# Moving attention probabilities into place inside SBUF instead of through DRAM, in a PE-bound three-stage kernel

## The chip, the core and the metric

The kernel runs on one NeuronCore of a Trainium2 chip. The metric is the device time of one execution in microseconds (us). A run of the profiler gives, beside that, a trace of every instruction; its clock starts at the first instruction of the program, and the time from there to the last is called the span.

## The reference

Three stages follow each other. The first is attention within chunks of 64 rows (8 batches, 8 heads, 576 rows, head size 64); its output becomes a matrix x of 4608 rows and 512 columns. The second is a feed-forward layer with a softplus, the third one with a maximum over three products.

```
scores = scale * np.matmul(q_c, k_c.transpose(0, 1, 2, 4, 3))      # 64 x 64 per chunk
scores = scores - np.max(scores, axis=-1, keepdims=True)
attn = np.exp(scores)
attn = attn / (np.sum(attn, axis=-1, keepdims=True) + 1e-09)
out = np.matmul(attn, v_c)
...
x = np.ascontiguousarray(attn_out.transpose(0, 2, 1, 3)).reshape(B * S, H * D)
h = x @ w_in                                  # 4608 x 512 by 512 x 2048
x = (np.maximum(h, 0.0) + np.log1p(np.exp(-np.abs(h)))) @ w_out
h = np.maximum(np.maximum(x @ w1, x @ w2), x @ w3)   # three times 512 x 768
out = h @ w_out
```

## The kernel before

The 4608 rows are nine blocks of 512. A block of x is made from four attention tiles, one for each pair of heads, so there are 36 tiles; the first eight (`attention_first`) run at the start, the other 28 (`attention`, tiles 8 to 35) are spread between the matmuls of the second stage. Blocks 0 to 2 go through that stage directly (`mlp1`, matmuls on lines 807 and 839); blocks 3 to 8 go in pairs with fewer, prepared products (`UnitA` on line 1135, `mlp1_out` on 1434, `Sevens` on 1280 and 1357). The third stage (`Triple`, lines 1582 and 1680) closes the program. The weights of the later products are sums and differences that the kernel computes itself and keeps in DRAM: `combos` writes them as `wso` (POOL, line 1248), `weights3` as `w2c` (POOL, line 940).

Nothing in the program order is written by hand. Every piece of work is an operation with a cost, a due time, what it reads and writes, and a latency `lat`; `Plan.order` runs through a model of the engines, always takes the waiting operation with the earliest due time, chooses between VectorE and ScalarE for the copies that may run on either, and hands out buffers as the model says they come free. The order in which operations start in that model is the order in which each engine's queue is filled. A change of one cost or latency therefore moves many instructions and changes which buffer each one gets. The large SBUF buffers are 46 places, s0 to s45, of 128 partitions by 4 KB; a name such as s14_268 is place s14, and 268 the running number of the buffer that got it.

In `attention`, tile t loads q, k and v (lines 445 and 470, on SP and POOL), transposes q and k on VectorE (lines 700, 701), and then one group of small TensorE matmuls, `products` (line 505, and 599 in the later tiles, which are called with `apart`), does two things: the scores of tile t and the product of the probabilities of tile t-2 with its v. The softmax follows on VectorE and ScalarE (line 564 and around it). The probabilities then have to be transposed. VectorE's transpose (line 753) does it within blocks of 32 by 32 and writes the lower half `pt` of a buffer PT; blocks that belong in another group of 32 partitions have to be carried there. Before the change `pt` is stored to a DRAM tile `pd` (line 757) and read back into the upper half `pT` by four loads, one for each group of 32 partitions (line 762), all issued by SP. `products` of tile t+2 reads `pT` and v.

Every queue runs its instructions in order: a DMA that waits on SP or POOL holds back all that stands behind it there, and a cast that waits on ScalarE all casts behind it.

Of the kernel before, what the change touches and what calls it, by code (L numbers as in the profile page):

```python
# [185 lines left out]
def tile_kernel(ctx: ExitStack, tc: tile.TileContext, q, k, v, w_in, w_out, w1, w2, w3, wo2, out):  # L186
    nc = tc.nc
    B, H, S, D = q.shape
# [3 lines left out]
    CH = 64  # L192
# [4 lines left out]
    TB = 512  # L197
    NB = NT // TB
    NC = TB // CH
    NTILE = NB * HP  # L200
# [68 lines left out]
    def slot(*kinds, shape=[P, 2, TB], dt=F32R):  # L269
        return Buf(*kinds, fresh=lambda i: slot_at(i, shape, dt))  # L270
# [5 lines left out]
    op = plan.op  # L276

    def copy_op(dst, src, r, w, psum=False, n=1.0, engs="DA", **kw):
        cost = {"D": 0.69 if psum else 0.43, "A": 0.58 if psum else 0.62}

        def fn(e):
            if e == "A":
                nc.scalar.copy(dst(), src())  # L283
            else:
                nc.vector.tensor_copy(dst(), src())

        return op({e: cost[e] * n for e in engs}, fn, r=r, w=w, **kw)
# [399 lines left out]
    def attention(t, after=(), apart=False):  # L687

        if t < NTILE:
# [4 lines left out]
            QK = slot("qh", "z", dt=F32)  # L694
# [8 lines left out]
        old = before.pop(0) if len(before) == 2 or t >= NTILE else None  # L703

        def products(e):
# [11 lines left out]
        o = op(  # L717
            {"P": 0.5 * ((old is not None) + (t < NTILE)) + 0.4},
            products,
            r=([old[1]] + [(old[2], n) for n in range(4)] if old else []) + ([(QK, "q"), (QK, "k")] if t < NTILE else []),  # L720
            w=parts,
            alloc=first_of(XZ) if apart else [G],
            after=last_t[-1:],
# [27 lines left out]
        PT = slot(*("vh", "z", "w")[:2 + (t > 2 * HP + 3)], dt=F32)  # L751
        pt, pT = half(PT, 0), half(PT, 1)
        op({"D": 0.69}, lambda e: nc.vector.transpose(
            pt().rearrange("p (b u i) -> p b u i", b=2, i=32), pbuf.t.rearrange("p (u b i) -> p b u i", b=2, i=32)
        ), r=[pbuf], w=[(PT, "pt")], alloc=[PT])
        pd = Buf("pd")
        op({"S": 0.48}, lambda e: nc.sync.dma_start(out=pd.t, in_=pt()), r=[(PT, "pt")], w=[pd], alloc=[pd], lat=8.0 if apart else 4.5)
        for n in range(4):
            c, b = divmod(n, 2)
            op(  # L760
                {"S": 0.48},
                lambda e, n=n, c=c, b=b: nc.sync.dma_start(
                    out=pT()[n * 32:(n + 1) * 32, :].rearrange("j (a f) -> j a f", a=2),
                    in_=pd.t[c * CH:(c + 1) * CH, b * (TB // 2):(b + 1) * (TB // 2)].rearrange("(a j) f -> j a f", a=2),
                ),
                r=[pd],
                w=[(PT, n)],
                lat=8.0 if apart else 4.5,
            )
        before.append((t, Rv, PT, vv))  # L770

# [696 lines left out]
    def first_of(z):  # L1468
        return [z] if z.first is None else []
# [244 lines left out]
    def strassen():  # L1714
# [11 lines left out]
        def group():  # L1726
            nonlocal tile_at
            if tile_at <= NTILE + 1:
                attention(tile_at, [first_loads[11]], True)
            tile_at += 1  # L1730
# [108 lines left out]
    for n, f in enumerate((1.0, -1.0)):  # L1839
        op(  # L1840
            {"D": 0.2},
            lambda e, n=n, f=f: nc.vector.tensor_scalar(eye.t[:, n, :P], ident, f, None, ALU.mult),
            w=[(eye, n)],
            alloc=[] if n else [eye],
            after=[made],
# [14 lines left out]
    for n, (b, j, first, last) in enumerate(steps):  # L1860
        if n >= NJ and n % (NJ // HP) == 0:
            t = HP + n // (NJ // HP)
            t = 2 * HP + (n - NJ) // 2
            while tiles <= t + 1 and tiles < 22:
                attention(tiles, [first_loads[tiles if tiles < 2 * HP + 3 else NJ - 1]])
                tiles += 1
        h = mlp1(b, j, first, last)
        if (b, j) in BEFORE:
            early(next(earlies), T0 + STEP * (n + EARLY), [h])
        if ("step", b, j) in COMBOS:  # L1870
            combos(COMBOS.index(("step", b, j)), [h], T0 + STEP * (n + 4))
        if b == NP - 1 and j % 2 == 0:
            weightsa(j // 2, [before_last], lead)
        if (b, j) == (1, NJ // 2):
            lead = h
        before_last = h if j % 2 == 0 else before_last
# [38 lines left out]
```

## Time and profile before

| what | value |
|---|---|
| median of 3 runs | 1366.23 us (1363.91 to 1366.64) |
| profiled execution, its own time | 1367.74 us |
| its span | 1365.9 us |
| TensorE (PE) busy | 1331.4 us, 97% |
| VectorE (DVE) busy | 984.5 us, 72% |
| ScalarE (ACT) busy | 545.4 us, 40% |
| mean granted TensorE clock | 0.998 |
| DMA packets | 289.38 MB |

The profiled execution has 1.84 us outside its span, and is 1.51 us above the median of the runs. PE is busy almost all the time, so what can change the time is the little that PE waits, and whether its clock is granted in full while it works.

### The profile page before, as it was taken

How to read it: one execution, taken by the hardware profiler on the slowest of the kernel's cores; microseconds unless marked ns; L12 is line 12 of the kernel's file. 1: busy time of each engine (PE TensorE's matmuls, PEld its weight loads, DVE VectorE, ACT ScalarE, POOL GpSimd, SP SyncE). 2: the span in 40 equal slices, each digit the busy share in tenths (PEclk: the TensorE clock that was granted, in tenths of full speed). 3: DMA queues.
4: the chain of work that ended last, by engine and by line, in shares of the span. 5: the costliest groups of instructions: out<-in, count | busy, mean ns of one | idle time of the engine just before them, and what ended most of it. 6: DMA issues, size and time to landing. Idle time of an engine off the chain costs nothing.

```text
span 1365.9 us, 23075 instructions
## 1 busy us (share of the span) xinstructions
PE 1331.4 (97%) x8616; PEld 1091.9 (80%) x8616; DVE 984.5 (72%) x1526; ACT 545.4 (40%) x1200; POOL 320.2 (23%) x561
## 2 busy tenths in 40 slices
PE   6899999999999998999999999999999999999998
PEld 4688888888888887887888887888888888888887
DVE  7999956797476996667858898779714597145951
ACT  5544434464544644535644454432113222132211
POOL 2011555532233324323221122121101121011100
PEclk9999999999999999999999999999999999999999
DMA  8565567677688899878967789655644465344401
GB/s 268 161 179 157 135 194 195 190 264 231 182 259 252 257 294 293 280 254 283 386 199 247 263 308 333 237 185 200 234 138 153 155 246 186 142 150 154 139 24 69
DMA packets 218863, 289.38 MB, mean 212 GB/s; under 512 B 121600, under 2 KB 146624, under 8 KB 218752
## 3 DMA queue, kind: packets, MB, share of 16 engines
q0 software_dynamic: 53792, 178.26, 37.7%
q1 hardware_dynamic: 159536, 100.48, 25.1%
q10 hardware_dynamic: 5424, 9.18, 1.8%
q8 instruction: 68, 1.11, 0.3%
q14 instruction: 43, 0.35, 0.1%
HBM read 196.61 MB, written 91.23 MB: 211 GB/s over the span
## 4 chain that ended last, share of the span: by engine, by line
PE 86%; issue 5%; DVE 3%; DMA 3%; POOL 2%; ACT 1%; SPq 0%; POOLq 0%; DVEq 0%; ACTq 0%
PE acc L1582 14%; PE both L1582 13%; PE acc L839 10%; PE ph L807 9%; PE acc L1434 8%; PE ph L1135 8%; PE both L1680 6%; PE one L1135 6%; PE acc L1680 5%; PE acc L1357 2%; PE ph L1357 2%; PE acc L1280 2%; PE aps L505 1%; PE one L599 1%; POOL rv L470 1%
## 5 line engine op out<-in xcount | busy, mean ns | idle before, releaser
L290 DVE TENSOR_TENSOR s<-s,s 128x1024 f32<-128x1024 f32 (+3 forms) x222 | 214.1, 994 | 9.7 <-ACT s L283 5.7
L1434 PE MATMUL acc<-g,s 128*128 128x512 f32 x768 | 185.0, 393 | 2.8 <-ACT tmp L283 1.9
L1434 PEld LDWEIGHTS acc<-g,s 128*128 128x128 f32 x768 | 143.1, 188 | 34.8 <-ACT tmp L283 2.3
L1135 PE MATMUL ph<-s,s 128*128 128x512 f32 x576 | 144.0, 389 | 0.7 <-ACT tmp L283 0.7
L807 PE MATMUL ph<-s,s 128*128 128x512 f32 x576 | 141.9, 395 | 1.6 <-DVE s L290 1.6
L839 PE MATMUL acc<-g,s 128*128 128x512 f32 x576 | 140.2, 392 | 0.1
L807 PEld LDWEIGHTS ph<-s,s 128*128 128x128 f32 x576 | 108.2, 190 | 25.8 <-DVE s L290 2.2
L1135 PEld LDWEIGHTS ph<-s,s 128*128 128x128 f32 x576 | 108.0, 188 | 23.5 <-ACT tmp L283 1.1
L839 PEld LDWEIGHTS acc<-g,s 128*128 128x128 f32 x576 | 107.2, 188 | 23.3 <-DVE g L290 0.4
L283 ACT CAST s<-s 128x512 fp32r<-128x512 f32 (+1 forms) x104 | 85.5, 835 | 96.9 <-DVE s L1613 31.2
L1582 PE MATMUL acc<-s,s 128*128 128x512 f32 x452 | 120.3, 389 | 0.0
L1565 POOL DMA_DIRECT2D s<-w2c x105 | 56.3, 537 | 266.6 <-PE acc L1582 80.7
L283 ACT CAST g<-s 128x1024 fp32r<-128x1024 f32 (+1 forms) x62 | 57.5, 929 | 146.9 <-PE both L1582 37.3
L1582 PE MATMUL acc<-g,s 128*128 128x512 f32 x400 | 110.0, 389 | 0.0
L1135 PE MATMUL one<-s,s 128*128 128x512 f32 x432 | 106.3, 389 | 0.2 <-ACT p L564 0.2
L1582 PE MATMUL both<-s,s 128*128 128x512 f32 x400 | 106.3, 389 | 0.0
L290 DVE TENSOR_TENSOR g<-tmp,g 128x512 fp32r<-128x512 f32 x104 | 70.8, 683 | 40.9 <-ACT g L283 40.7
L1582 PE MATMUL both<-g,s 128*128 128x512 f32 x368 | 100.1, 389 | 0.0
L1582 PEld LDWEIGHTS acc<-s,s 128*128 128x128 f32 x452 | 84.9, 188 | 17.6
L1135 PEld LDWEIGHTS one<-s,s 128*128 128x128 f32 x432 | 81.0, 188 | 17.4 <-ACT p L564 0.6
L1582 PEld LDWEIGHTS both<-s,s 128*128 128x128 f32 x400 | 75.1, 188 | 15.6
L1582 PEld LDWEIGHTS acc<-g,s 128*128 128x128 f32 x400 | 75.1, 188 | 15.6
(163 smaller groups left out, 2144.5 us busy)
## 6 DMA issues: line engine op xcount, KB each, us to landing
s<-w2c POOLq DMA_DIRECT2D x105, 512.0 KB, 4.4
s<-wac POOLq DMA_DIRECT2D x66, 512.0 KB, 6.3
w2c<-s POOLq DMA_DIRECT2D x45, 512.0 KB, 5.0
wac<-s POOLq DMA_DIRECT2D x24, 512.0 KB, 5.4
s<-in_moe_w_dram POOLq DMA_DIRECT2D x18, 512.0 KB, 5.2
s<-x2d POOLq DMA_DIRECT2D x18, 512.0 KB, 5.7
s<-in_moe_w_in_dram SPq DMA_DIRECT2D x16, 512.0 KB, 4.5
s<-in_moe_w_out_dram SPq DMA_DIRECT2D x16, 512.0 KB, 5.5
```

The source lines that it names most:

```text
L283: nc.scalar.copy(dst(), src())
L290: return op({"D": 0.69 * n}, lambda e: nc.vector.tensor_tensor(dst(), a(), b(), f), r=r, w=w, **kw)
L470: dma(out=dst().rearrange("p (c e d) -> p c e d", e=2, d=D)[half * CH:(half + 1) * CH, lo:lo + mine, h, :], in_=v[b, t % HP * 2 + h].rearr ...
L807: nc.tensor.matmul(ph.t, w[:, wi, kk * P:(kk + 1) * P], x[kk].t[:, xi], start=(kk == 0 and wi == 0 and xi == 0), stop=(kk == KD - 1 and wi ...
L839: nc.tensor.matmul(acc[m // 2].t[:, m % 2], w[:, wi, m * P:(m + 1) * P], g.t[:, gi, :], start=(first and wi == 0 and gi == 0), stop=(last ...
L1135: nc.tensor.matmul(dst(), ws.t[:, wi, col + kk * P:col + (kk + 1) * P], x[kk].t[:, xi], start=(first and kk == 0 and wi == 0 and xi == 0), ...
L1280: nc.tensor.matmul(u.acc[f].t[:, m], w.t[:, wi, m * P:(m + 1) * P], g.t[:, gi, :], start=(first and wi == 0 and gi == 0), stop=(last and w ...
L1357: nc.tensor.matmul(dst(m), lhs(wi, nn, m), (GH, GL)[gi].t[:, nn], start=(fresh and nn == 0 and wi == 0 and gi == 0), stop=(nn == 1 and wi ...
L1434: nc.tensor.matmul(acc[half].t[:, m % 2], w.t[:, wi, m * P:(m + 1) * P], g.t[:, gi, :], start=(first and wi == 0 and gi == 0), stop=(last ...
L1565: lambda e, k=k, z=z: nc.gpsimd.dma_start(out=z.t.bitcast(F32), in_=w2c[s][late + k]),
L1582: nc.tensor.matmul(bank.view()[:, f], ws(wi, slice(f * HT + kk * P, f * HT + (kk + 1) * P)), (XH, XL)[xi].t[:, kk], start=(first and kk == ...
L1680: nc.tensor.matmul(banks[t // 2].view()[:, t % 2], (GH, GL)[gi].t[:, f, t * P:(t + 1) * P], wo2_of[j].t[:, wi], start=(j == 0 and wi == 0 ...
```

## The change

Tiles 8 to 35 no longer use the DRAM tile. ScalarE copies the whole `pt` (128 partitions by 512 values) to `pT`; half of the blocks are in place with that. Then SP issues four transfers from SBUF to SBUF, each of 32 partitions by 256 values (32 KB), that put the other half where they belong, over what the copy left there. Each of the four waits for the copy, since both write the same buffer. `products` now waits for the copy and the four transfers. The model's latency for a transfer is 2.6 us, or 3.5 in the later tiles, where the store and the loads had 4.5 and 8.0 each.

```
-            r=([old[1]] + [(old[2], n) for n in range(4)] if old else []) + ([(QK, "q"), (QK, "k")] if t < NTILE else []),
+            r=([old[1]] + [(old[2], n) for n in (*range(4), "pT")] if old else []) + ([(QK, "q"), (QK, "k")] if t < NTILE else []),
...
-        pd = Buf("pd")
-        op({"S": 0.48}, lambda e: nc.sync.dma_start(out=pd.t, in_=pt()), r=[(PT, "pt")], w=[pd], alloc=[pd], lat=8.0 if apart else 4.5)
+        copied = copy_op(pT, pt, [(PT, "pt")], [(PT, "pT")], engs="A")
         for n in range(4):
             c, b = divmod(n, 2)
+            to, of = (slice((2 * c + x) * 32, (2 * c + x + 1) * 32) for x in (b, 1 - b))
             op(
                 {"S": 0.48},
-                lambda e, n=n, c=c, b=b: nc.sync.dma_start(
-                    out=pT()[n * 32:(n + 1) * 32, :].rearrange("j (a f) -> j a f", a=2),
-                    in_=pd.t[c * CH:(c + 1) * CH, b * (TB // 2):(b + 1) * (TB // 2)].rearrange("(a j) f -> j a f", a=2),
+                lambda e, to=to, of=of, b=b: nc.sync.dma_start(
+                    out=pT()[to, (1 - b) * (TB // 2):(2 - b) * (TB // 2)], in_=pt()[of, b * (TB // 2):(b + 1) * (TB // 2)]
                 ),
-                r=[pd],
+                r=[(PT, "pt")],
                 w=[(PT, n)],
-                lat=8.0 if apart else 4.5,
+                after=[copied],
+                lat=3.5 if apart else 2.6,
             )
```

Since the plan is made anew, the order moves in many places. From about 340 us on, PE's own order of products is the same in both; what moves is the work of the other engines around it, and who gets which buffer. Three places are shown.

**First place.** On PE, some 200 us into the program, stands the product of the tile whose probabilities are in buffer s45_112 (lines 505, 807 and 839 are attention, first and second product of `mlp1`). Before:

```order
L839 MATMUL acc0_95<-g2_77,s23_84_1823 128x512 x6
L839 MATMUL acc1_96<-g2_77,s23_84_1823 128x512 x6
L807 MATMUL ph1_93<-s36_53_1230,s11_97_2137 128x512 x3
L807 MATMUL ph1_93<-s37_55_1292,s11_97_2137 128x512 x3
L807 MATMUL ph1_93<-s38_58_1369,s11_97_2137 128x512 x3
L807 MATMUL ph1_93<-s39_60_1408,s11_97_2137 128x512 x3
L839 MATMUL acc0_95<-g0_75,s5_90_1948 128x512 x6
L839 MATMUL acc1_96<-g0_75,s5_90_1948 128x512 x6
L505 MATMUL aps0_94<-s45_112_2775,tmp2_80 64x64 x16
L505 MATMUL aps0_94<-s43_110_2687 64x64 x16
```

PE at the same place with the change:

```order
L839 MATMUL acc0_95<-g2_77,s23_84_1823 128x512 x6
L839 MATMUL acc1_96<-g2_77,s23_84_1823 128x512 x6
L505 MATMUL aps0_94<-s45_112_2775,tmp3_81 64x64 x16
L505 MATMUL aps0_94<-s43_110_2687 64x64 x16
L807 MATMUL ph1_93<-s36_53_1230,s11_96_2129 128x512 x3
L807 MATMUL ph1_93<-s37_55_1292,s11_96_2129 128x512 x3
L807 MATMUL ph1_93<-s38_58_1369,s11_96_2129 128x512 x3
L807 MATMUL ph1_93<-s39_60_1408,s11_96_2129 128x512 x3
L839 MATMUL acc0_95<-g0_75,s5_89_1949 128x512 x6
L839 MATMUL acc1_96<-g0_75,s5_89_1949 128x512 x6
```

The attention group has moved ahead of two blocks of twelve large matmuls, one of line 807 and one of line 839. On SP the transfers for the same buffer stood so before (line 445 loads q, 470 v, 757 and 762 are the store and the loads of the probabilities):

```order
L445 DMA tmp8_86<-in_q_dram 32x8x32 x7
L757 DMA pd0_90<-s45_112_2775 128x512
L470 DMA rv0_88<-in_v_dram 64x64
L470 DMA rv0_88<-in_v_dram 64x4x64
L445 DMA tmp8_86<-in_q_dram 32x8x32
L445 DMA rq0_74<-in_q_dram 32x8x32 x4
L762 DMA s45_112_2775<-pd0_90 32x2x256 x4
```

and with the change:

```order
L445 DMA tmp5_83<-in_q_dram 32x8x32 x7
L470 DMA rv0_88<-in_v_dram 64x3x64
L762 DMA s45_112_2775<-s45_112_2775 32x256 x4
L445 DMA tmp5_83<-in_q_dram 32x8x32
L445 DMA rq0_74<-in_q_dram 32x8x32 x6
```

The four transfers have moved up past one load of v and five of q, and still stand behind the seven loads of q.

**Second place.** On POOL, some 515 us into the program, stand the last stores of `combos` (line 1248, `wso0_3` to `wso3_3`) between loads of v (line 470) and of prepared weights (line 1060). Before:

```order
L1248 DMA wso3_2_242<-s6_260_6000 128x1024
L1060 DMA s1_265_6062<-wac2_0_161 128x1024
L470 DMA rv0_88<-in_v_dram 64x4x64 x2
L470 DMA rv0_88<-in_v_dram 64x3x64 x2
L470 DMA rv0_88<-in_v_dram 64x64 x2
L1248 DMA wso0_3_231<-s14_268_6126 128x1024
L1060 DMA s29_271_6171<-wac2_2_163 128x1024
L1248 DMA wso1_3_235<-s6_270_6161 128x1024
L1248 DMA wso2_3_239<-s17_272_6185 128x1024
L1060 DMA s27_274_6209<-wac2_1_162 128x1024
L1060 DMA s2_275_6246<-wae1_180 128x1024
L1248 DMA wso3_3_243<-s14_273_6196 128x1024
```

and with the change:

```order
L1248 DMA wso3_2_242<-s27_261_5978 128x1024
L1060 DMA s6_264_6009<-wac1_1_159 128x1024
L1060 DMA s20_266_6066<-wac2_0_161 128x1024
L1248 DMA wso0_3_231<-s1_265_6030 128x1024
L470 DMA rv0_88<-in_v_dram 64x4x64 x2
L470 DMA rv0_88<-in_v_dram 64x3x64 x2
L470 DMA rv0_88<-in_v_dram 64x64 x2
L1248 DMA wso1_3_235<-s27_268_6081 128x1024
L1248 DMA wso2_3_239<-s14_269_6120 128x1024
L1248 DMA wso3_3_243<-s39_270_6135 128x1024
L1060 DMA s1_273_6180<-wac2_2_163 128x1024
```

The store of `wso0_3` has moved ahead of the six loads of v. Before, `wso0_3` and `wso3_3` use the same place, s14, so the second can only be written when the store of the first has landed; with the change they use s1 and s39. The earlier user of s39 is a buffer inside `combos` that is never stored. `wso1_3` follows `wso3_2` in one place in both (s6, now s27).

**Third place.** The stores of `weights3` (POOL, line 940), some 640 us into the program. Before:

```order
L940 DMA w2c1_0_186<-s24_323_7189 128x1024
L940 DMA w2c2_0_189<-s11_324_7192 128x1024
L940 DMA w2c3_0_192<-s38_325_7227 128x1024
L1060 DMA s7_328_7264<-wac1_0_158 128x1024
L940 DMA w2c4_0_195<-s33_329_7267 128x1024
L1060 DMA s14_331_7313<-wac1_2_160 128x1024
L940 DMA w2c5_0_198<-s39_332_7316 128x1024
L940 DMA w2c6_0_201<-s43_333_7319 128x1024
L940 DMA w2c7_0_204<-s20_337_7366 128x1024
L940 DMA w2c8_0_207<-s38_338_7380 128x1024
L940 DMA w2c9_0_210<-s35_339_7394 128x1024
L940 DMA w2c10_0_213<-s33_340_7417 128x1024
```

and with the change:

```order
L940 DMA w2c1_0_186<-s40_339_7412 128x1024
L940 DMA w2c2_0_189<-s31_340_7415 128x1024
L940 DMA w2c3_0_192<-s40_341_7458 128x1024
L940 DMA w2c4_0_195<-s31_343_7488 128x1024
L940 DMA w2c5_0_198<-s20_344_7493 128x1024
L940 DMA w2c6_0_201<-s40_345_7524 128x1024
L940 DMA w2c7_0_204<-s31_346_7534 128x1024
L940 DMA w2c8_0_207<-s20_347_7557 128x1024
L940 DMA w2c9_0_210<-s43_348_7566 128x1024
L940 DMA w2c10_0_213<-s40_349_7571 128x1024
```

These stores used eight places, and now four: s40 is used by w2c1, w2c3, w2c6 and w2c10. On ACT the casts that fill these buffers stand between the casts that fill the three buffers g0 to g2, each of which feeds one block of `mlp1_out`. With the change the stretch from the first to the last buffer in s40 reads so there:

```order
L283 CAST s40_339_7412<-s8_332_7295 128x512
L283 CAST s31_340_7415<-s8_332_7295 128x512
L283 CAST g2_77<-tmp4_82 128x512
L283 CAST g1_76<-tmp1_79 128x512
L283 CAST g0_75<-tmp3_81 128x512
L283 CAST s40_341_7458<-s34_330_7293 128x512
L283 CAST g2_77<-tmp7_85 128x512
L283 CAST s39_342_7479<-s43_292_6619 128x512
L283 CAST s31_343_7488<-s34_330_7293 128x512
L283 CAST s20_344_7493<-s32_329_7292 128x512
L283 CAST g1_76<-tmp6_84 128x512
L283 CAST g0_75<-tmp5_83 128x512
```

```order
L283 CAST s40_345_7524<-s34_330_7293 128x512
L283 CAST s31_346_7534<-s32_329_7292 128x512
L283 CAST g2_77<-tmp8_86 128x512
L283 CAST s20_347_7557<-s34_330_7293 128x512
L283 CAST s43_348_7566<-s34_330_7293 128x512
L283 CAST g1_76<-tmp0_78 128x512
L283 CAST s40_349_7571<-s32_329_7292 128x512
```

The two pieces follow each other without a gap. Eight casts to g stand between the first cast to s40 and the last; before, the casts that fill the `weights3` buffers stood earlier among them, and in other places.

## Rows read from the trace of the kernel before

**Rows 1.** The page, section 1: busy us (share of the span) and instructions.
```profile
PE 1331.4 (97%) x8616; PEld 1091.9 (80%) x8616; DVE 984.5 (72%) x1526; ACT 545.4 (40%) x1200; POOL 320.2 (23%) x561
```

**Rows 2.** Waits of PE, 102 to 1300 us: us in total, times, longest.
```profile
PE one L599 <- DVE tmp L290: 5.2, 1, 5.2
...
PE aps L505 <- DMA s<-pd: 0.6, 1, 0.6
```

**Rows 3.** Windows by stage: length, busy time of PE, PEld, DVE, ACT, POOL; clock, DMA share, GB/s.
```profile
102.00:340.00 238.00, 237.25 (x1858) 193.70 (x1857) 191.26 (x395) 112.09 (x364) 100.76 (x171) 1.00 0.68 196
340.00:700.00 360.00, 351.10 (x2348) 286.38 (x2347) 261.16 (x490) 177.98 (x486) 106.26 (x178) 1.00 0.83 265
```

**Rows 4.** Timeline of PE, 203 to 222 us: start, us, instructions, [idle before].
```profile
204.74 0.69 PE L505 MATMUL aps<-s,tmp 64*64 64x64 f32 x32
...
214.18 2.88 PE L807 MATMUL ph<-s,s 128*128 128x512 f32 x12
...
220.82 0.63 PE L505 MATMUL aps<-s,tmp 64*64 64x64 f32 x27 [0.63 <-DMA s<-pd]
```

**Rows 5.** Timeline of SP's queue, 202 to 222 us: start, us, DMA issues.
```profile
202.20 8.90 SPq L445 DMA_DIRECT2D tmp<-in_q_dram  x7
...
212.24 2.15 SPq L470 DMA_DIRECT2D rv<-in_v_dram  x2
...
217.12 1.82 SPq L762 DMA_DIRECT2D s<-pd  x4
```

**Rows 6.** Timeline of DVE, 198 to 222 us: the transpose of these probabilities.
```profile
205.59 0.71 DVE L753 STREAM_TRANSPOSE s<-p 128x512 f32<-128x512 f32 x1
```

**Rows 7.** Tile pd, 132 to 340 us: issue to landing of its DMAs.
```profile
DMA to landing us min/median/max: 1.7/2.6/6.7
```

**Rows 8.** Chain of waits, 517 to 540 us: start, us, what.
```profile
521.84 1.87 issue
...
525.37 6.05 DMA wso<-s
...
531.44 0.63 ACT s L283
...
532.70 0.69 DVE tmp L290
...
533.43 2.08 PE one L599 x62
535.52 3.48 PE acc L1434 x12
```

**Rows 9.** Chain of waits of the whole run: the same groups of matmuls elsewhere.
```profile
540.36 2.72 PE acc L1434 x12
...
651.11 0.62 PE one L599 x32
```

**Rows 10.** Windows of 10 us, columns as in the windows by stage.
```profile
530.00:540.00 10.00, 6.57 (x82) 5.65 (x83) 7.22 (x15) 5.66 (x23) 1.93 (x3) 0.83 1.01 379
...
640.00:650.00 10.00, 7.54 (x30) 5.18 (x29) 7.89 (x14) 6.22 (x13) 4.37 (x9) 1.00 0.77 242
...
660.00:670.00 10.00, 10.00 (x46) 8.29 (x45) 8.88 (x16) 6.24 (x11) 1.60 (x3) 1.00 1.04 412
```

**Rows 11.** Tile wso, whole run: issue to landing, stores and loads together.
```profile
DMA to landing us min/median/max: 3.5/5.9/9.4
```

**Rows 12.** Timeline of ACT, 640 to 700 us, one cast.
```profile
645.82 0.62 ACT L283 CAST s<-s 128x512 fp32r<-128x512 f32 x1 [3.20 <-DMA w2c<-s]
```

**Rows 13.** Tile w2c, 640 to 700 us: issue to landing of its 15 stores.
```profile
DMA to landing us min/median/max: 2.9/10.5/15.6
```

**Rows 14.** Groups of ACT, 132 to 640 us: busy us, mean ns, idle before.
```profile
L283 ACT COPY tmp<-ph 128x512 f32<-128x512 f32 x42 | 24.9, 592 | 16.9 <-PE ph L1135 15.8
```

**Rows 15.** Window 132 to 640 us, ACT alone: length, busy, clock, DMA share, GB/s.
```profile
132.00:640.00 508.00, 245.56 (x759) 1.00 0.79 239
```

**Rows 16.** Waits of SP's queue, whole run.
```profile
SPq L762 <- DMA pd<-s: 39.8, 14, 5.0
```

## The prediction

> **What bounds the kernel now.** The page comes first: TensorE (PE) is busy for 97% of the span, and the next engine for 72% [rows 1]. The mean of the granted clock is full, so the matmuls themselves can't be made shorter by moving probabilities about; only PE's waits can change. So I read the windows by stage. The attention tiles that change run from 132 us, when the first store to `pd` is issued, to about 640 us, so what happens before 102 us (start-up) and after 700 us is the same work in both. Between 102 and 340 us PE is idle for 238 - 237.25 = 0.75 us, between 340 and 700 us for 360 - 351.10 = 8.9 us [rows 3]. Then the list of PE's waits, for what ends them: the transfers of the probabilities end one wait, of 0.6 us, in the whole run, and the largest wait, 5.2 us, is ended by a VectorE addition in front of an attention group [rows 2]. So the round trip through DRAM is hidden nearly everywhere. A tile's probabilities are needed two tiles later, and that covers it. What the change saves in latency is therefore worth 0.6 us at most by itself; the rest of the argument is about how the new plan moves the work around PE's few waits.
>
> **The wait for the probabilities (first place).** Before, PE reaches the product of s45_112 after 219.9 us and starts it in earnest at 220.82, with 0.63 us of idle put down to the transfer [rows 4]. The transfer is late because SP is: seven loads of q take SP 8.90 us to issue, from 202.20 to 211.1, and only behind them come the store and, at 217.12, the four loads, 1.82 / 4 = 0.46 us each [rows 5]. With the change the four transfers stand behind the same seven loads and one load of v (2.15 / 2 = 1.07 us): they start at 211.1 + 1.07 = 212.2, and the last is issued at 212.2 + 3 x 0.46 = 213.6. ScalarE's copy is done by then, since the transpose ends at 206.3 [rows 6]. How long 32 KB from SBUF to SBUF take no row shows; the nearest are the 64 KB loads from `pd` in this stretch, 1.7 us at the least, 2.6 in the median, 6.7 at the most [rows 7]. By the median the data is there at 216.2. But the new order brings PE to this product two blocks earlier, where the block of 214.18 started [rows 4]. PE would wait 216.2 - 214.2 = 2.0 us instead of 0.63: **+1.4 us** (ends +0.5 and +5.5 by 1.7 and 6.7).
>
> A rule speaks against transfers of this form: by the Trainium skill, "SBUF — State Buffer", section "Door 1: The DMA port swizzle", a transfer over 32 partitions reaches only 8 of the 16 ports to SBUF, about 218 GB/s, and the section "The DMA setup-cost knee" adds about 2 us that no size takes away. An estimate from that page is 32 KB / 218 GB/s + 2 = 2.15 us for each; PE would wait 213.6 + 2.15 - 214.2 = 1.6 us, and the sum below would be 0.4 us lower. The rows' 2.6 us, with other transfers in flight, is the value that I use.
>
> In all other tiles I cost the latency at nothing: what hides it is the work of two tiles, and the new path, one copy of 0.59 us and transfers like those of [rows 7], is shorter than a store, its landing and four loads.
>
> **The big wait (second place).** The chain of waits tells what the 5.2 us are [rows 8]. POOL comes late to the store of `wso0_3`, because loads of v ahead of it hang in the queue (the chain's "issue", 1.87 us in the row shown). The store leaves at 525.37 and takes 6.05 us to land; only then may ScalarE cast the next sum into the same place s14 (531.44), VectorE subtracts, and behind that in VectorE's order stands the addition (532.70) for which PE waits. And PE pays twice: after the wait the granted clock of 530 to 540 us is 0.83 [rows 10], and 62 small matmuls take 2.08 us where 32 take 0.62 elsewhere, twelve large ones 3.48 where they take 2.72 [rows 8, 9]. That is (2.08 - 2 x 0.62) + (3.48 - 2.72) = 1.6 us. With the change this chain can't form: `wso0_3` is issued before the loads of v, and `wso3_3` goes into s39, which waits for no store. So 5.2 + 1.6 goes: **-6.8 us** (ends -6.8 and 0, if another wait comes in its place). One handover of that kind stays, `wso3_2` to `wso1_3` in s27, and its cast now stands ahead of ScalarE's copies that clear the attention banks. A `wso` transfer lands in 5.9 us in the median and 9.4 at the most [rows 11]. Of this late end, 9.4 - 5.9 = 3.5 us, I take a small part, since of the sixteen `wso` buffers PE's list of waits shows only the one handover above [rows 2]: **+0.5 us** (0 to 3.5).
>
> **The stores of `weights3` (third place).** In 640 to 650 us PE is idle for 10 - 7.54 = 2.5 us [rows 10]. At 645.82 ScalarE casts into a place whose `w2c` store had to land first, 3.20 us of waiting [rows 12], and the casts that feed PE stand behind it. With the change `weights3` starts later, after these casts: **-2.5 us** (0 to -2.5). But then it runs with four places instead of eight, in the middle of the casts to g. Between the first and the last cast to s40 lie three handovers, each a cast of 0.62 us [rows 12], a subtraction of 0.69 [rows 8] and the landing L of a store. In the same stretch stand eight casts to g, each for one block of twelve matmuls, 2.72 us [rows 9]: PE has 8 x 2.72 = 21.8 us of work, and with three g buffers at most two blocks, 5.4 us, more in hand. PE waits when 3 x (1.31 + L) is over 27.2 us, that is from L = 7.8 on. Before, these stores landed in 2.9 us at the least, 10.5 in the median and 15.6 at the most [rows 13], while the DMA engines were full (share 1.04, 412 GB/s) [rows 10]. With four places, fewer stores can be in flight at a time, so they queue less behind each other; but loads of stored activations share the engines. I take L = 8.5, below the median: 3 x 9.81 - 27.2 = **+2.2 us** (0 for L up to 7.8; +8.2 for 10.5).
>
> **What is hidden.** ScalarE gets 28 copies. The nearest row is its copy from PSUM of the same size, 0.592 us [rows 14], so 16.6 us in all, against 508 - 245.56 = 262 us in which it is idle between 132 and 640 us [rows 15]: 0. Without that cover each copy would cost its 0.59 us. SP issues four DMAs per tile instead of five, and its 39.8 us of waiting for the store to `pd` [rows 16] become a wait for the copy; behind the waiting transfers stand loads of q, k, v and of stored activations, all due much later, so this counts as 0 too. DMA traffic loses 28 x 512 KB and gains 28 x 128 KB, about 11 MB in 508 us at 239 GB/s [rows 15], that is 9% of the traffic there. It can only shorten landings; I give it no term of its own.
>
> **Sum.** +1.4 - 6.8 + 0.5 - 2.5 + 2.2 = -5.2 us. The span would be 1365.9 - 5.2 = 1360.7 us, the profiled execution 1362.5. That execution is 1.5 us above the median of the runs, so the forecast for the median is 1366.2 - 5.2 = 1361.0 us. A difference under 0.2% (2.7 us) can't be told from none here.
>
> **Rivals.** *Slower: `weights3` becomes the bound.* If the stores land as late as when the engines were full, three handovers in one place hold back the casts to g. With L = 12, between the median and the maximum of [rows 13], the third place costs 3 x 13.31 - 27.2 = 12.7 us instead of 2.2: -5.2 + 10.5 = +5.3, 1371.5 us. It decides (slower by over 2.7 us) from 10.1 us at this place on, L = 11.1. For it speaks the median of 10.5; against it that this was with eight places in use. Chance 0.14.
>
> *No change: the big wait comes back under another name.* The stretch is as full as before, and s27's handover holds up the copies that clear the banks as s14's held up the addition. If PE waits for it as it did, 5.2 us, the sum is 0: 1366.2 us. For it: landings of up to 9.4 us. Against it: its store no longer stands behind the loads of v. Chance 0.22. That the change does nothing at all, since the latency was hidden, has the same time.
>
> *More: the new waits are hidden as well.* Transfers land in under 2 us and `w2c` stores in under 7.8: what remains is -0.6 - 6.8 - 2.5 = -9.9, 1356.3 us. Chance 0.18.
>
> **Numbers.** The forecast's case has 0.46, with its own range of 1358 to 1364 us. Faster: 0.44 of it and the last rival, 0.62. Within 0.2%: the third case and the edges, 0.23. Slower: 0.15. The range goes from 1355 us, a little under the last rival, to 1370 us, which leaves out most of the slower case.
>
> **What would show it.** PE's wait at 528 us gone, and the granted clock full from 520 to 550 us; a wait for the transfer of s45_112 near 214 us of 1 to 3 us; no wait at 641 to 650 us, and one of about 2 us between 670 and 690 us behind casts that wait for `w2c` stores; ScalarE's copies off the chain. I am wrong if the 28 copies or SP's transfers appear in PE's list of waits at several tiles, or if a new wait of over 5 us stands at a place that I haven't named.

## The result and the profile after

The changed kernel takes 1374.85 us in the median (1370.29 to 1377.01, five runs); the kernel before took 1366.64 us on the same chip (1363.91 to 1367.36). The ratio is 1.0054, with a 95% interval of 1.0028 to 1.0079: slower, by more than the 0.2% that can be told from no change, and outside the forecast range. The profiled execution is one of the quickest of the five: 1370.57 us, span 1368.8.

Section 1 of its page; columns as in [rows 1]:

```profile
PE 1332.7 (97%) x8616; PEld 1092.0 (80%) x8616; DVE 985.5 (72%) x1528; ACT 558.6 (41%) x1226; POOL 319.3 (23%) x557
```

ScalarE has 13.2 us more to do, and PE the same work. Next the waits of PE from 102 to 1300 us, which answer to [rows 2]:

```profile
PE acc L1434 <- ACT g L283: 3.6, 2, 2.6
PE acc L1434 <- DVE g L290: 2.6, 4, 0.9
PE aps L505 <- DMA s<-s: 2.3, 2, 1.4
...
PE ph L1135 <- ACT tmp L283: 1.2, 1, 1.2
PE one L599 <- DVE tmp L290: 1.2, 1, 1.2
```

The 5.2 us wait is gone. The second product (line 1434) now waits 6.2 us for g (casts and additions together), where the list of the kernel before has only

```profile
PE acc L1434 <- DVE g L290: 1.0, 3, 0.4
```

Where the waits stand is seen from the windows, columns as in [rows 3]; the first two answer to [rows 3], the others to [rows 10]:

```profile
102.00:340.00 238.00, 235.72 (x1794) 192.94 (x1794) 191.15 (x392) 119.56 (x377) 99.74 (x169) 1.00 0.60 172
340.00:700.00 360.00, 351.16 (x2407) 284.86 (x2406) 259.09 (x487) 185.47 (x500) 105.28 (x176) 1.00 0.79 245
530.00:540.00 10.00, 10.00 (x104) 8.14 (x103) 7.36 (x15) 5.82 (x12) 3.69 (x7) 1.00 1.03 304
640.00:650.00 10.00, 9.91 (x44) 7.84 (x44) 10.00 (x19) 4.76 (x9) 4.54 (x8) 1.00 0.80 224
```

PE's idle time from 340 to 700 us is 8.84 us against 8.90 before, although both waits that the forecast removed are gone (530 to 540 us is full and 640 to 650 us nearly so, at the full clock). As much has come elsewhere. PE's timeline shows four places (start, us, instructions, idle before):

```profile
217.19 0.29 PE L505 MATMUL aps<-s,tmp 64*64 64x64 f32 x2 [1.44 <-DMA s<-s]
218.32 0.63 PE L505 MATMUL aps<-s,tmp 64*64 64x64 f32 x27 [0.84 <-DMA s<-s]
...
488.15 0.50 PE L1434 MATMUL acc<-g,s 128*128 128x512 f32 x1 [2.64 <-ACT g L283]
...
501.26 3.94 PE L1434 MATMUL acc<-g,s 128*128 128x512 f32 x16 [0.86 <-DVE g L290]
...
634.20 0.79 PE L599 MATMUL one<-s,rv 64*64 64x64 f32 x32 [1.15 <-DVE tmp L290]
...
657.85 0.50 PE L1434 MATMUL acc<-g,s 128*128 128x512 f32 x1 [0.97 <-ACT g L283]
658.99 25.24 PE L1434 MATMUL acc<-g,s 128*128 128x512 f32 x107 [0.64 <-DVE g L290]
```

**At 214 us** stands the wait for the transfers that the forecast named. SP shows why it is longer (timeline of its queue, columns as in [rows 5]):

```profile
204.27 9.00 SPq L445 DMA_DIRECT2D tmp<-in_q_dram  x7
213.37 0.66 SPq L470 DMA_DIRECT2D rv<-in_v_dram  x1
214.30 2.44 SPq L762 DMA_DIRECT2D s<-s  x4
...
471.62 3.87 SPq L445 DMA_DIRECT2D rk<-in_k_dram  x8
475.59 0.39 SPq L883 DMA_DIRECT2D w2d<-tmp  x1
476.09 2.42 SPq L762 DMA_DIRECT2D s<-s  x4
478.55 2.85 SPq L795 DMA_DIRECT2D x2d<-tmp  x4
481.45 3.21 SPq L1415 DMA_DIRECT2D tmp<-gd  x4
```

**At 488 us** stands a place that the forecast did not name. The reloads of stored activations (`gd`, line 1415) leave SP from 481.45 on, behind eight loads of k, four transfers and four stores of x, one issue right after the other. In the kernel before the first of these reloads left six microseconds earlier (timeline of its SP queue), while PE came only 3.5 us earlier to the block in front of the wait:

```profile
475.48 0.45 SPq L1415 DMA_DIRECT2D tmp<-gd  x1
```

In the changed kernel ScalarE's cast of g waits for one of them (timeline of ACT), and PE for the cast:

```profile
487.48 1.15 ACT L283 CAST g<-tmp 128x512 fp32r<-128x512 f32 x2 [4.14 <-DMA tmp<-gd]
```

**At 634 us** it is POOL. In the changed kernel's chain of waits a load of raw weights (line 320) stands behind loads of v that hang in the queue; VectorE's conversion of the weights (line 334) waits for it, and behind that in VectorE's order stands the addition (633.55) for which PE waits. This is the form of the old wait at 528 us, in another place:

```profile
619.84 4.03 issue
623.87 1.03 POOL rv L470 x2
...
627.03 5.12 DMA s<-in_moe_w_dram
...
632.18 0.43 DVE tmp L334
...
633.55 0.60 DVE tmp L290
```

**At 658 us** a cast to g stands on ScalarE behind a cast that waits for a load of converted weights (`w2d`, line 908; timeline of ACT):

```profile
656.38 0.62 ACT L283 CAST s<-s 128x512 fp32r<-128x512 f32 x1 [4.75 <-DMA s<-w2d]
```

The three loads of `w2d` start on POOL from 648.39 us on and land in 10.5 us in the median; in the kernel before they start from 623.68 us on and land in 4.8 us.

### The profile page after: what moved, and what is told of

Read it like the earlier page. It is cut to its first block, busy times and chain, and to the rows that moved or that the text cites. A ratio compares the mean times of both kernels' runs of the same rounds, so it can differ in the third digit from the quotient of the medians.

```text
span 1368.8 us, 23085 instructions
## 1 busy us (share of the span) xinstructions
PE 1332.7 (97%) x8616; PEld 1092.0 (80%) x8616; DVE 985.5 (72%) x1528; ACT 558.6 (41%) x1226; POOL 319.3 (23%) x557
## 4 chain that ended last, share of the span: by engine, by line
PE 86%; DVE 6%; DMA 4%; issue 3%; ACT 1%; SPq 1%; POOL 0%; DVEq 0%; ACTq 0%; POOLq 0%
PE acc L1582 14%; PE both L1582 13%; PE acc L839 10%; PE ph L807 9%; PE ph L1135 9%; PE acc L1434 7%; PE one L1135 6%; PE both L1680 6%; PE acc L1680 5%; PE acc L1357 2%; DVE s L290 2%; PE ph L1357 2%; PE acc L1280 2%; PE aps L505 1%; DVE tmp L290 1%
```

## The experiments

Each run was timed in five rounds beside the kernel before, whose medians beside the four sets of runs were 1366.38, 1366.20, 1366.19 and 1366.65 us.

**Theories.** A: the new order makes the loss, by late hand-overs at places that the forecast did not price. C: the transfers inside SBUF, or ScalarE's copies, cost the time themselves. "Order" means here the plan's order together with the buffers that it hands out. B, for the changed kernel alone: it is start-up, where the clock differs between executions.

### The changed kernel again

> The changed kernel once more, as it is. Its five runs lay between 1370.3 and 1377.0 us and the profiled one was among the lowest, so its trace may show too little. Theory A (the new order of SP's queue brings the reloads of stored activations, tile gd, too late to PE near 485 us, by an amount that depends on how transfers land): a median of 1372 to 1376 us again, and PE's wait for a cast or addition to g near 488 us in the trace, 2.5 us or more. Theory B (the loss comes from start-up, where the granted clock was 0.95 and 0.90 in the first two stretches of 34 us): the same median, but the place near 488 us small and start-up long.

Measured: 1373.36 us (1368.66 to 1375.40), ratio 1.0046 [1.0030, 1.0062]. The profiled execution has a span of 1371.6 us, near the median of its runs. Its waits of PE:

```profile
PE one L599 <- DVE tmp L290: 3.0, 1, 3.0
PE acc L1434 <- ACT g L283: 2.9, 1, 2.9
PE acc L1434 <- DVE g L290: 2.2, 3, 1.1
PE aps L505 <- DMA s<-s: 2.2, 1, 2.2
```

The same places as at 214, 488 and 634 us; at 214 us the waits add up to 3.1 us (0.9 of them put to issue) instead of 2.3. At 634 us the wait is 3.0 us instead of 1.2. From 630 to 640 us PE is idle for 3.0 us and the granted clock is 0.83, and the 32 small matmuls behind the wait take 1.23 us instead of 0.79. Its two start-up windows had clocks of 1.00 and 0.95, better than in the first trace, yet it is slower. PE reaches the same matmul at the end of start-up (number 1505, at 102.8 us in the kernel before) 1.0 us sooner than the kernel before did, and takes 6.8 us longer from there to its last one: B falls.

### Order and transfers apart

e2 has the changed kernel's order and the old way through DRAM, at the same places of the order:

```
-        copied = copy_op(pT, pt, [(PT, "pt")], [(PT, "pT")], engs="A")
+        pd = dram.tile([P, TB], F32, name=f"pdx{t}"); copied = op({"A": 0.62}, lambda e: nc.sync.dma_start(out=pd, in_=pt()), r=[(PT, "pt")], w=[(PT, "pT")])
```

and the four loads of before in the four transfers' lambdas. e3 is the opposite, the old order with the copy where the store was, and the four transfers in the four loads' lambdas:

```
-        op({"S": 0.48}, lambda e: nc.sync.dma_start(out=pd.t, in_=pt()), r=[(PT, "pt")], w=[pd], alloc=[pd], lat=8.0 if apart else 4.5)
+        op({"S": 0.48}, lambda e: nc.scalar.copy(pT(), pt()), r=[(PT, "pt")], w=[pd], alloc=[pd], lat=8.0 if apart else 4.5)
```

> The order of the changed kernel, but the probabilities go through DRAM as before (the copy is replaced by the store, the four transfers by the four loads, at the same places of the order). Theory A, that the order alone makes the loss: within 3 us of the changed kernel in the same call, so 1372 to 1378 us, with the wait near 488 us; the product near 214 us waits longer than with the new transfers, 3 to 5 us instead of 2. Theory C, that the transfers inside SBUF or ScalarE's copies cost the time: 1361 to 1367 us, since the order itself should then bring what was forecast.

> The order of the kernel before, but the new copy stands on ScalarE where the store was on SP, and the four transfers inside SBUF where the loads were. Theory A (order): the time of the kernel before, less at most 0.6 us for the one wait that the transfers ended, so 1365 to 1367 us, with the 5.2 us wait near 528 us still there. Theory C (the transfers cost): 1372 to 1378 us.

Measured: e2 1389.37 us (1388.22 to 1392.79), ratio 1.0172 [1.0151, 1.0192]; e3 1363.76 us (1360.06 to 1368.12, twelve runs), ratio 0.9980 [0.9966, 0.9994]. C falls: the new transfers by themselves make the kernel 2.6 us faster. The order is the loss, 1373.36 - 1363.76 = 9.6 us with the new transfers. e2 is a miss: that it lies 16 us above the changed kernel, and not within 3, says that the new order leaves less time for this path than the way through DRAM takes. So its 23 us over the kernel before are no measure of the order alone. PE's waits in e2 begin with

```profile
PE aps L505 <- DMA s<-pdx: 5.9, 2, 4.9
```

(The plan of e2 also has no time on SP for the store and none for its landing; what this adds was not measured.) The trace of e3 is its slowest execution, 1368.12 us; start-up takes 2.6 us longer in it than in the kernel before, and the rest 2.4 us less. In it the wait at 528 us is still there, as expected, but 3.4 us long instead of 5.2:

```profile
PE one L599 <- DVE tmp L290: 3.4, 1, 3.4
```

### The second place alone, and with the new transfers

e4 is the kernel before, e8 is e3, each with this edit, which moves six loads of v behind the store of `wso0_3` on POOL:

```
-        for o in plan.order():
+        listed = plan.order()
+        i = listed.index(store["s", 0, 3]) + 1
+        late_v = [o for o in listed[:i] if o.eng == "G" and any(z.kinds[0] == "rv" for z in o.bufs)][-6:]
+        listed = [o for o in listed[:i] if o not in late_v] + late_v + listed[i:]
+        for o in listed:
```

> The kernel before, with six loads of v on POOL moved behind the store of wso0_3; nothing else is moved. If the big wait near 528 us hangs on this order, as the forecast has it for the second place: 5.2 to 6.8 us less than before, 1359.5 to 1361.5 us, the granted clock full from 530 to 540 us. Rival, the wait comes back under another name (the next store or the cast behind it): 1365 to 1367 us with a wait of 3 us or more between 525 and 540 us.

> The old order with the new copy and transfers, and with the six loads of v behind the store of wso0_3. The two gains are 2.6 and 2.4 us of 1366.4. If they add: 1361 to 1362 us. If they come from the same wait (PE's at 528 us, which was 3.4 us instead of 5.2 with the new transfers alone): 1363 to 1364 us.

Measured: e4 1364.01 us (1362.02 to 1367.47), ratio 0.9985 [0.9972, 0.9997]; e8 **1361.07 us** (1359.43 to 1361.82), ratio 0.9958 [0.9946, 0.9971], faster than both kernels. In e4 the wait at 528 us is gone and the window from 530 to 540 us, which answers to [rows 10], is full:

```profile
530.00:540.00 10.00, 10.00 (x46) 8.28 (x45) 6.02 (x13) 4.74 (x20) 1.90 (x3) 1.00 1.02 344
```

Its waits of PE now begin with

```profile
PE one L599 <- DMA rv<-in_v_dram: 2.0, 3, 1.0
PE acc L1434 <- ACT tmp L283: 1.5, 1, 1.5
```

So 2.0 us of waits for the loads of v themselves have come (0.4 at 528, the rest near 546 us), and 2.4 us are left of the 5.2 to 6.8. The gains of e3 (2.6) and e4 (2.4) add in e8, 1366.20 - 1361.07 = 5.1 us, within the noise; they are not quite separate, since part of e3's comes from the wait at 528 us (3.4 us instead of 5.2) that e4's edit removes. Its waits of PE of 1 us and more:

```profile
PE acc L1434 <- DVE g L290: 2.3, 3, 1.7
PE acc L1357 <- issue: 1.0, 1, 1.0
```

and its window that answers to the second of [rows 3]:

```profile
340.00:700.00 360.00, 355.98 (x2375) 289.99 (x2374) 262.28 (x489) 189.73 (x504) 107.98 (x181) 1.00 0.79 254
```

4.0 us of idle time are left in this stretch, and the window from 102 to 340 us is full.

### The three places of the new order

Here the changed kernel's list is edited behind the planner. One loop moves operations, by their numbers, behind another:

```
+        listed = plan.order()
+        for first, last, behind in [(2411, 2418, 2322)]:
+            some = [o for o in listed if first <= o.n <= last and o.eng in "SG"]
+            rest = [o for o in listed if o not in some]
+            i = rest.index(plan.ops[behind]) + 1
+            listed = rest[:i] + some + rest[i:]
-        for o in plan.order():
+        for o in listed:
```

e5 has this triple (eight loads of k behind three reloads of `gd`), e6 has (2733, 2736, 2762) (four loads of v behind the load of raw weights), e7 has both and (1064, 1070, 889) (seven loads of q behind the four transfers at 214 us). e9 has (2113, 2138, 2322), of which it moves the transfers and the stores of x. f1 has the triples of e9, e6 and the one of 214 us.

> The changed kernel, with eight loads of k on SP moved behind the next three reloads of stored activations (tile gd); their issue took 3.87 us right ahead of them. If SP's lateness makes PE's waits between 485 and 503 us (2.6 to 2.9 us at 488, 0.9 at 501): these waits gone and 3 to 5 us less than the changed kernel's 1373.4, so 1368.5 to 1370.5 us. If the landing of the reloads makes them, whatever the time of their issue: 1372 to 1375 us and a wait for a cast to g of over 2 us in the same place.

> The changed kernel, with four loads of v on POOL moved behind the load of raw weights that follows them near 627 us. If this load, late behind loads of v that hang in POOL's queue, makes PE's wait at 634 us (1.2 us in one trace, 3.0 in the other, and matmuls at a lower clock behind the longer one): that wait gone, 2 to 4 us less than 1373.4, so 1369.5 to 1371.5 us. Rival: the loads of v become late instead, and PE waits at 650 us or behind it: within 1 us of 1373.4.

> The changed kernel with both moves, and a third: the seven loads of q on SP, 9 us of issue, go behind the four transfers of the probabilities for which PE waits near 214 us. If the loss of the new order is these three places: 3 to 5, 2 to 4 and 2 to 4 us less, 7 to 12 together, so 1362 to 1366.5 us, as low as the new transfers in the old order (1363.8). If the loss is spread over the order: no more than 4 us less, 1369 us or above.

> The changed kernel; on SP the four transfers of one tile and the four stores of x that follow them (4.4 to 5.3 us of issue, all due much later) go behind the next three reloads of stored activations, and the loads of k stay where they are. Moving the loads of k (e5) had only exchanged one late transfer for another. If the loss at 485 to 503 us is a matter of what stands ahead of the reloads on SP: the wait at 488 us gone with nothing in its place before 505 us, 3 to 5 us less than the changed kernel in the traces, 1369 to 1371 us. If SP's queue is full there whatever the order: a wait of 2 us or more still stands between 480 and 505 us, and the time is 1372 to 1374 us.

> The changed kernel with three moves: the seven loads of q behind the transfers (214 us), the four transfers and the stores of x behind the reloads (485 us, as in e9), the loads of v behind the load of raw weights (634 us). If the three places are the loss: 1364 to 1367 us, 6 to 9 us less than the changed kernel, and no wait of PE over 2 us in the trace. If moves only pass the lateness on: 1368 to 1371 us, as with the first three moves (1369.0).

Measured: e5 1372.95 us (1369.97 to 1373.66); e6 1371.96 (1371.05 to 1372.91); e7 1368.97 (1366.37 to 1371.42); e9 1370.37 (1367.83 to 1376.85, too wide to rank); f1 1367.39 (1365.18 to 1372.81), ratio 1.0014 [1.0000, 1.0028].

e5 is a miss. The wait at 488 us goes, and the next block of PE waits 3.3 us instead, for an addition to g. The chain of waits names the landing of a load of k there, but VectorE works without a gap from 485.14 us, before that landing, up to this addition, and the transpose in between (line 700) is one of q. What VectorE waits for just before 485.14 us is the landing of a `wso` store (its list of waits, 480 to 490 us):

```profile
DVE s L285 <- DMA wso<-s: 2.7, 1, 2.7
```

With the loads of k left in place (e9) 1.6 us remain at the same block, and VectorE waits 1.0 us for the same landing:

```profile
DVE s L285 <- DMA wso<-s: 1.0, 1, 1.0
```

e7 and f1 have this wait too (2.1 and 1.1 us); in the three traces where the reloads stay late (the change, e1, e6) VectorE has none for it in this stretch. So the stretch has a second late hand-over right behind the first. In e6 PE's wait at 634 us is 0.5 us, and the median 1.4 us lower, less than the runs of e1 scatter. Less than expected comes through; the load of raw weights, now ahead of the loads of v, is held up itself: POOL stands for 4.37 us before it. e7 fell between its two expectations. Only at 214 us does a move settle its place: from 102 to 340 us PE is full in e7 and f1. What f1 says is bounded: the three places hold 1373.36 - 1367.39 = 6.0 of the 9.6 us. Its largest wait is 1.8 us, in the stretch at 485 us; at 652 us PE waits 1.1 and 0.6 us for g, as the changed kernel does at 658 us, and no edit touched that place. What is left of each place in f1's trace is in the table of the next section. f1 fell just above its expected 1364 to 1367.

### Other plans

If the loss were in latencies that are too short (L), longer ones would mend it. If the old order is a good draw among plans whose model knows neither hanging queues nor landings under load (P), any new plan should be worse. The edits change latencies of the plan alone: `lat=3.5 if apart else 2.6` of the changed kernel becomes 8.0/4.5 (e10), 4.5/3.5 (e11) and 3.0/2.3 (f4); `lat=8.0 if apart else 4.5` of the kernel before becomes 7.5/4.2 (e12) and 8.5/5.0 (f2); in f3 `GDLAT`, the latency of the reloads, becomes 8.5.

> The changed kernel planned with the old latencies, 8.0 and 4.5 us for each transfer, instead of 3.5 and 2.6. Theory L (the order loses because the plan takes transfers for faster than they land): about as good as the new transfers in the old order, 1362 to 1366 us. Theory P (every new plan falls on other late hand-overs, since the plan's model knows neither the hanging of queues nor landings under load): any time from 1364 to 1376 us, with its largest waits of PE at places where neither kernel had one.

> The changed kernel planned with 4.5 and 3.5 us for each transfer, a little more than the change's 3.5 and 2.6. Theory L: between the changed kernel and e10, 1366 to 1372 us. Theory P: any time from 1364 to 1376 us, not in the order of the latencies, and other places of PE's waits.

> The kernel before, with its transfers through DRAM, planned with latencies of 7.5 and 4.2 us instead of 8.0 and 4.5. What the transfers do is unchanged; only the plan is made anew. Theory L: within 1.5 us of the kernel before, 1365 to 1368 us. Theory P: 1368 to 1378 us, since the old plan is one of the better draws.

> The kernel before, planned with latencies of 8.5 and 5.0 us for its store and loads instead of 8.0 and 4.5. Theory P (any new plan is a draw, and the old one is a good draw): 1369 us or more. Theory L (longer latencies are safe): 1364 to 1368 us.

> The kernel before, with 8.5 us instead of 8.0 as the plan's latency for the reloads of stored activations; nothing about the probabilities is changed. Theory P: 1369 us or more. Theory L: 1364 to 1368 us.

> The changed kernel planned with 3.0 and 2.3 us for each transfer instead of 3.5 and 2.6. Theory P: anywhere from 1366 to 1386 us. Theory L: a little slower than the changed kernel, 1373 to 1377 us, with longer waits for the transfers.

| plan | transfers | median, us | range, us |
|---|---|---|---|
| of before, 8.0/4.5 | DRAM | 1366.65 | 1360.99 to 1372.27 |
| e12, 7.5/4.2 | DRAM | 1384.68 | 1382.18 to 1387.91 |
| f2, 8.5/5.0 | DRAM | 1382.20 | 1381.01 to 1389.88 |
| f3, reloads 8.5 | DRAM | 1378.97 | 1378.37 to 1382.69 |
| of the change, 3.5/2.6 | SBUF | 1373.36 | 1368.66 to 1375.40 |
| f4, 3.0/2.3 | SBUF | 1370.72 | 1366.14 to 1377.00 |
| e11, 4.5/3.5 | SBUF | 1385.81 | 1383.79 to 1386.53 |
| e10, 8.0/4.5 | SBUF | 1377.29 | 1373.23 to 1381.71 |

L falls: the times do not go with the latency, and half a microsecond more or less costs the kernel before 12 to 18 us though its transfers stay the same. P has the sign in all six, every new plan being slower than the old one; its bounds were too narrow (e10, e11 and e12 lie above them). But the six are no independent draws. f4 has the changed kernel's own places and no other of 1.2 us or more. The largest waits of the other five are where neither kernel had one of 1 us, and two of them recur: 4.9 to 6.7 us near 655 us, in e10, e11, e12 and f2, and 7.2 us in the third stage, whose work no edit touched, in e11, e12, f2 and f3. In e12 (waits of PE):

```profile
PE acc L1582 <- ACT s L283: 7.2, 1, 7.2
PE acc L1434 <- ACT tmp L283: 6.4, 1, 6.4
```

With the lower clock behind it (0.74 and 0.75 from 870 to 890 us in e12) the wait in the third stage costs these four 10.2 to 11.4 us, counted over the same 600 matmuls. So of the 12 to 18 us by which e12, f2 and f3 are slower, some 11 are this one event, and the rest is 1 to 7. In each of the four ScalarE's copy, for which PE waits, starts 0.08 us after the fifth of seven VectorE additions in a row has ended, behind 9.6 us of idle time for which the trace names no releaser; that it waits for this addition is not shown.

## Why the prediction was wrong

The traces allow a count by place. PE runs 8616 matmuls in each kernel, in the same order but for numbers 1648 to 2707 (the first place) and a few swaps of neighbours. So the time from one numbered matmul to another can be compared with the kernel before, idle time and lower clock together (differences in us, one execution each, computed from the starts of the matmuls; the times are those of the kernel before):

| matmuls | at, us | forecast | first trace of the change | e1 | e8 | f1 |
|---|---|---|---|---|---|---|
| to 1505, start-up | to 103 | 0 | +1.8 | -1.0 | +0.3 | +0.9 |
| to 3000, first place | 103 to 298 | +1.4 | +1.2 | +3.4 | -1.4 | -1.4 |
| 3000 to 4100 | 298 to 442 | 0 | 0.0 | 0.0 | 0.0 | 0.0 |
| to 4600, wait at 488 us | 442 to 517 | 0 | +5.5 | +5.8 | 0.0 | +3.3 |
| to 4850, second place and s27 | 517 to 554 | -6.3 | -6.7 | -6.7 | -6.7 | -6.7 |
| to 5350 | 554 to 628 | 0 | -0.5 | -0.2 | +0.8 | -0.3 |
| to 5420, wait at 634 us | 628 to 637 | 0 | +1.3 | +4.6 | +0.5 | +1.5 |
| to 5480, third place | 637 to 651 | -2.5 | -3.1 | -3.2 | -0.5 | -3.3 |
| to 5720, third place | 651 to 704 | +2.2 | +3.4 | +2.4 | 0.0 | +3.9 |
| to the last | 704 to 1361 | 0 | 0.0 | +0.8 | 0.0 | 0.0 |
| behind start-up | | -5.2 | +1.1 | +6.8 | -7.3 | -2.9 |

The places that the forecast named come to -5.2 and -4.1 us in the two traces of the change, against -5.2 (in the third place partly by luck, as said below). The two that it did not name, at 488 and 634 us, cost 6.8 and 10.4 us, and they turn the gain into a loss. The two executions of the same program differ by 5.7 us behind start-up, most of it at 214 and 634 us.

**The step that failed** stands under what is hidden: SP's wait becomes a wait for the copy, and "behind the waiting transfers stand loads of q, k, v and of stored activations, all due much later, so this counts as 0 too". The reloads of stored activations were not due much later: PE waits 2.64, 0.22 and 0.86 us for g between 488 and 502 us, 3.7 us that the sum has at 0, and the whole stretch takes 5.5 us longer. The wider fault is that the sum had three places because three places of the order had been read, and everything that the new plan moved elsewhere counted as 0. The 634 us place, 1.3 and 4.6 us, was lost in the same way, in POOL's queue. That the new order loses 9.6 us is shown by e3 against e1, that 214, 485 and 634 us hold 6.0 of them by f1. Point by point:

- **+1.4, first place.** Right in mechanism. The waits are 1.44 + 0.84 = 2.3 us in the first trace and 3.1 in the second (2.17 for the transfer, 0.90 put to issue), against 0.63; the stretch takes 1.2 and 3.4 us longer, so the size fits the first trace and is too small for the second. The transfers left SP at 214.30, not 212.2, because the loads of q ahead of them started 2.1 us later (PE came 1.6 us later itself), and each takes 0.6 us to issue, not 0.46. Their landing was well taken: from 132 to 340 us 1.8 us at the least, 2.6 in the median, 6.7 at the most, against an assumed 2.6. The rule of the Trainium skill ("SBUF — State Buffer", sections "Door 1: The DMA port swizzle" and "The DMA setup-cost knee") that gave an estimate of 2.15 us lies between the least and the median of these landings; no run here shows whether ports or queues make the rest.
- **-6.8, second place.** Right: gone, with the clock full from 530 to 540 us, and worth 6.7 us in the count. The chain was the right one, as e4 shows, which cut it and nothing else; and e4 also shows that the loads of v are then late themselves in the old order.
- **+0.5, s27.** Did not show: no wait of PE from 520 to 545 us.
- **-2.5 and +2.2, third place.** The first is right as far as it goes: the wait at 641 to 650 us is gone. The second has about the right size, but that is luck. The `w2c` stores land sooner than assumed (tile w2c, 640 to 700 us),

```profile
DMA to landing us min/median/max: 2.9/5.1/7.6
```

and by the forecast's own sum PE waits only from L = 7.8 on, where it took 8.5. The chain does lead over such a store, which lands in 7.51 us, and ScalarE's cast behind it:

```profile
667.32 7.51 DMA w2c<-s
...
674.91 0.63 ACT s L283
```

It ends in a wait before 686.80 us that the kernel before has too, at 683.90, and that is only half a microsecond longer:

```profile
686.80 1.65 PE L1135 MATMUL ph<-s,s 128*128 128x512 f32 x6 [1.22 <-ACT tmp L283]
```

```profile
683.90 1.66 PE L1135 MATMUL ph<-s,s 128*128 128x512 f32 x6 [0.68 <-ACT tmp L283]
```

The larger part, 0.97 + 0.64 us at 658 us, comes behind a load of `w2d` that the forecast did not look at.
- **0 for the copies.** Right: 28 copies of 0.624 us, 17.5 us, none of them on PE's list of waits.
- **0 for SP.** Wrong, as said; and four DMAs instead of five were no relief. The change's take 0.588 us each in the median to issue, against 0.426 for a load from `pd` and 0.345 for the store: 4 x 0.588 = 2.35 us a tile, against 4 x 0.426 + 0.345 = 2.05. The rows are those of line 762 in the change and in the kernel before:

```profile
L762 SPq DMA_DIRECT2D s<-s x112: 507/588/1593, 138.0 to 638.5; - x112
```

```profile
L762 SPq DMA_DIRECT2D s<-pd x112: 303/426/1943, 137.4 to 635.4; - x112
```

Of the rivals none had the cause. The one on the slower side put it on late landings of `weights3`' stores, which came sooner than the forecast had them. The one of a wait that comes back under another name was nearest: the form came back exactly, at 634 us, not in s27.

## What to carry to other kernels

A change inside a planned program is two changes, what it does and a new draw of the whole order; run the new operation in the frozen old order first (e3: 2.6 us faster), and take what the whole change does beyond that as the price of the order (9.6 us). The old operation in the new order (e2) does not separate the two, for the new plan gives it too little time. If the plan is made anew, price the new order over its whole length: for each queue, list what stands ahead of every transfer that PE needs soon, not only at the places where the old profile had a wait. And when the order can be edited behind the planner, the new transfers and one move on a known order (e8, 5.1 us under the kernel before) are worth more than three repairs of a new one (f1, level with the kernel before).

## What was not expected of the hardware

- Transfers of 32 KB inside SBUF landed little sooner than the loads of 64 KB from DRAM on the same queue (both line 762): 2.6 us in the median from issue to landing against 2.8 from 132 to 340 us, and 3.4 against 4.6 from 340 to 640 us. From 102 to 340 us the DMA engines were also busy for less of the time (share 0.60 against 0.68). What the transfers save besides is the store and its landing, 4.0 us in the median for `pd`.
- The trace puts some of SP's waits down to landings that have nothing to do with the buffers of the DMA that waits: a load of q stood for 5.6 us at 465 us until a store of `gd`, issued by ScalarE, had landed. No run tested this. The kernel before has the same wait 2 us earlier, 4.4 us long. SP's waits there, in the changed kernel:

```profile
SPq L445 <- DMA gd<-tmp: 5.6, 1, 5.6
```

- POOL stands for 1 to 5 us before some of its DMAs, and the trace names no releaser for it ("issue": 4.03 and 4.93 us at 619.8 us in the two traces of the change, before loads of v). In e6, with the order turned, 4.37 us stand at the same time before the load of raw weights, so it is not the loads of v that are slow. The waits at 528 us in the kernel before and at 634 us in the changed one began so. What POOL waits for was not tested.
